# Loading w_in by half chunks, and a reordered start, in a float32 attention and feed-forward kernel

## The chip, the cores and the metric

The kernel runs on one core of one Trainium2 chip. The metric is the device time of one execution in microseconds (us), as the median of several runs. Engines are named as in the profile: PE is the matrix engine (PEld its weight loads), DVE the vector engine, ACT the scalar engine, POOL GpSimd, SP the queue that issues all DMAs here.

## The reference

A cross attention between tokens `x` (8 batches, 8 heads, 512 tokens, head size 64) and 32 state rows per head, in both directions, and then a feed-forward block on all 8 x 544 rows:

```
a  = softmax(scale * x @ state.T);   xread = a @ state        # 512 rows per batch
a2 = softmax(scale * state @ x.T);   sread = a2 @ x           # 32 rows per batch
y  = concat([xread, sread]) -> (4352, 512)
h  = y @ w_in                        # w_in  (512, 2048)
g  = h / (1 + exp(-1.702 h))
out = g @ w_out                      # w_out (2048, 512), out float32
```

`x` and `state` are float32. The weights arrive as 64-bit floating point numbers, so `w_in` is 8 MiB and each weight has to be turned into a float32 number on the chip.

## The kernel before

**What the matrix engine does.** Since `xread = a @ state`, the kernel never forms `xread`. For a batch b and a chunk c of 512 of the 2048 hidden columns it forms `M(b, c)`, the product of the state and of `w_in`'s chunk (`att_M`, L451: eight small matmuls that run beside each other, then two ACT copies out of PSUM, L460). `up_x(b, f)` (L529, `up` L520) multiplies 128 columns of M with the transposed softmax `aT` of the batch; ACT applies the activation (L527, "gelu" below). Four `up_x` use one chunk. Batches 0 and 1 are made this way at the start, chunk by chunk, while the weights still come in; the down projection and the other six batches follow, and the change leaves their order as it is.

**Pieces of weights.** `w_in` is loaded in 16 pieces of 512 KB (`PIECES` L166, `load_weight` L170): in chunk c, piece k is the 128 rows k of 512 columns, 4 KB a row. 16 pieces of `w_out` follow. A piece is turned into float32 by five DVE instructions and two on ACT: `mask` (L207) takes the exponent's bits; the "powers" or clamps (L218 and L219) are two ACT instructions on it; then DVE's `fraction` (L225), L236 (which needs the powers), L239 and L243. `powers_to(n)` brings masks and powers up to piece n, `round_to(n)` does the rest up to piece n and runs powers some pieces ahead. M(b, 0) needs the first four pieces, M(b, 1) the next four, and so on. Below, p0 to p15 are the pieces in order.

**The order.** The schedule is manual: each engine, and SP's queue of DMAs, runs its instructions in the order in which the code emits them (L1124 and below). SP issues p0 and p1, the state and x of batch 0, p2 and p3, the state and x of batch 1, then p4 and on. PE begins with `keep_warm` (L122: matmuls on zeros whose result nobody reads), turns x of batch 0 (`att_xT_arriving`), makes its scores, runs 24 more such matmuls, turns state and x of batch 1 (`att_state`, `att_xT`: 4 transposes of PE and an ACT copy for each of four head pairs), makes batch 1's scores (`att_scores`, L343), then M(0, 0), four `up_x` of batch 0, M(1, 0), four of batch 1, M(0, 1), and so on. The softmax of batch 0 is DVE's `att_x_norm(0)` (L403 to L408), which ends in `aT(0)`. That of batch 1 is `att_blocks(1)` (L351), `att_x_exp(1)` (L394, L395 and an exponential on ACT, L396) and `att_x_norm(1)`. Between exponentials and gelus ACT loads another table of functions (ACT_TABLE_LOAD).

**Buffers.** PSUM tiles come from two pools with two buffers each: "att" (transposes, most M) and "h" (`up_x`, warm matmuls; with `spare=True` M takes "h" and `up_x` takes "att"). A matmul group waits until ACT has read the tile that held its buffer.

Of the kernel before, what the change touches and what calls it, by code (L numbers as in the profile page):

```python
# [10 lines left out]
FP32 = mybir.dt.float32  # L11
I32 = mybir.dt.int32
U32 = mybir.dt.uint32
AF = mybir.ActivationFunctionType
# [6 lines left out]
def kernel(  # L21
# [30 lines left out]
    nc = tc.nc  # L52

    B, H, S, D = x.shape
# [3 lines left out]
    P = 128  # L58
    NPR = P // Ns
    NG = H // NPR  # L60
    NF = DF // P
    SCH = S // P
    ST = S + Ns
    FC = 512
    NFC = DF // FC
# [16 lines left out]
    mpool = ctx.enter_context(tc.tile_pool(name="mpool", bufs=1))  # L82
# [4 lines left out]
    psH = ctx.enter_context(tc.tile_pool(name="psH", bufs=2, space=bass.MemoryType.PSUM))  # L87
# [4 lines left out]
    def att_ps(shape, name):  # L92
        return psA.tile(shape, FP32, tag="att", name=name)
# [16 lines left out]
    low = konst.tile([P, 6, S], FP32, name="low")  # L110
# [11 lines left out]
    def keep_warm(n):  # L122
        ps = psH.tile([P, FC], FP32, tag="h", name="warm")
        for _ in range(n):
            nc.tensor.matmul(ps, zeros[:, :P], zeros, start=True, stop=True)  # L125
# [9 lines left out]
    def load_x(b):  # L135
        if b == 1:
            xn[b] = sums[:, 0].rearrange("p (c h d) -> p c h d", c=SCH, h=H)
        else:
            xn[b] = xpool.tile([P, SCH, H, D], FP32, tag="xn", name=f"xn_{b}")
        for c in range(SCH):  # L140
            nc.sync.dma_start(xn[b][:, c], x_v[b, c])
# [20 lines left out]
    w_in = [konst.tile([P, NPR, FC], FP32, name=f"w_in_{c}") for c in range(NFC)]  # L162
    w_out = konst.tile([P, NF, DM], FP32, name="w_out")
    w_in_words, w_out_words = moe_w_in.bitcast(I32), moe_w_out.bitcast(I32)

    PIECES = [("i", c, k) for c in range(NFC) for k in range(NPR)] + [("o", f) for f in range(NF)]  # L166
    raw, power, begun = {}, {}, {}
    AHEAD = 3

    def load_weight(i):  # L170

        key = PIECES[i]
        nin, room = NFC * NPR, NF // 2
        if i < room or nin - NPR <= i < nin:
            o = 2 * (i % room if i < room else i - (nin - NPR))
            raw[i] = w_out[:, o : o + 2].rearrange("p f n -> p (f n)").bitcast(I32)
        else:
            o = 2 * (i % 4)
            raw[i] = later[:, o : o + 2].rearrange("p f n -> p (f n)").bitcast(I32)
        if key[0] == "i":  # L180
            _, c, k = key
            src = w_in_words[P * k : P * (k + 1), 2 * FC * c : 2 * FC * (c + 1)]
        else:
            src = w_out_words[P * key[1] : P * (key[1] + 1)]
        nc.sync.dma_start(raw[i], src)

# [4 lines left out]
    for i, v in enumerate((8.0 * most, 8.0 * (most - least))):  # L193
        t = konst.tile([P, 1], FP32, name=f"edge_{i}")
        nc.gpsimd.memset(t, v)
        edge.append(t)

    def words(i):
        w = raw[i].rearrange("p (n w) -> p w n", w=2)
        return w[:, 0].bitcast(U32), w[:, 1]  # L200

    def mask(i):

        _, hi = words(i)
        sc = low[:, 2 + i % (AHEAD + 1)].bitcast(I32)
        power[i] = sc
        nc.vector.tensor_scalar(sc, hi, 0x7FF00000, None, ALU.bitwise_and)  # L207

    def round_a(i):
# [3 lines left out]
        sc = power[i]  # L213
        if PIECES[i][0] == "o":
            nc.vector.tensor_scalar(sc, sc, most, least, ALU.min, ALU.max)
# [5 lines left out]
    def fraction(i):  # L221

        key = PIECES[i]
        dst = w_in[key[1]][:, key[2]] if key[0] == "i" else w_out[:, key[1]]
        nc.vector.tensor_scalar(dst.bitcast(I32), words(i)[1], 0xFFFFF, 0x100000, ALU.bitwise_and, ALU.bitwise_or)  # L225
        begun[i] = dst

# [19 lines left out]
    def before(i):  # L247

        nin = NFC * NPR
        return i - (nin - NPR if i < nin else 2 * NPR if i < nin + NPR else NPR)  # L250

    def load_weights(upto):
        while done["load"] < min(upto, len(PIECES)):
            load_weight(done["load"])
            done["load"] += 1

    def powers_to(n):
        while done["a"] < min(n, len(PIECES)):
            load_weights(done["a"] + 1)
            round_a(done["a"])  # L260
            done["a"] += 1

    def round_to(n, ahead=AHEAD):

        nin = NFC * NPR
        while done["b"] < min(n, len(PIECES)):
            i = done["b"]
            powers_to(i + 1)
            round_b(i, min(i + 1 + ahead, max(nin, i + 1)), i + 1 < nin and (i + 1 < n or i >= NPR))
            done["b"] += 1  # L270
            while done["b"] > NPR and done["load"] < len(PIECES) and before(done["load"]) < done["b"]:
                load_weights(done["load"] + 1)
# [12 lines left out]
    A = {b: {} for b in range(B)}  # L285
# [29 lines left out]
    def by_state(b, ps, rhs):  # L315

        for j in range(NPR):
            for g in range(NG):
                rows, st = slice(D * g, D * (g + 1)), slice(Ns * j, Ns * (j + 1))
                nc.tensor.matmul(ps[g][st], A[b]["stT"][rows, st], rhs(rows, j), start=True, stop=True)  # L320
# [19 lines left out]
    def att_scores(b):  # L340
        a = A[b]
        a["s"] = bank_o[:NG] if b == 0 else bank_o[NG:]
        by_state(b, a["s"], lambda rows, j: a["xT"][rows, j])  # L343
# [54 lines left out]
    def att_x_norm(b):  # L398

        a = A[b]  # L400
        t = a["e1"].rearrange("p g i n -> p (g i) n")
        sm = apool.tile([P, NS1], FP32, tag="sm", name=f"sm_{b}")
        nc.vector.reduce_sum(out=sm, in_=t, axis=AX.X)  # L403
        nc.vector.tensor_scalar(sm, sm, eps, None, ALU.add)
        nc.vector.reciprocal(out=sm, in_=sm)
        nc.vector.tensor_tensor(out=t, in0=t, in1=sm.to_broadcast((P, NS1, Ns)), op=ALU.mult)
        a["aT"] = low[:, :NG] if b == 1 else apool.tile([P, NG, S], FP32, tag="aT", name=f"aT_{b}")
        nc.vector.transpose(  # L408
            a["aT"].rearrange("p g t -> p (g t)"), a["e1"].rearrange("p g i n -> p (g i n)")
        )  # L410
# [37 lines left out]

    turns = {"M": 0}

    def att_M(b, c, spare=False):  # L451

        m = mpool.tile([P, NG, FC], FP32, tag=f"M{turns['M'] % NFC if b < 2 else c}", name=f"M_{b}_{c}")
        turns["M"] += 1
        A[b]["M", c] = m
        name = f"M_{b}_{c}_"
        ps = [psH.tile([P, FC], FP32, tag="h", name=name + str(g)) if spare else att_ps([P, FC], name + str(g)) for g in range(NG)]
        by_state(b, ps, lambda rows, j: w_in[c][rows, j])
        for g in range(NG):
            nc.scalar.copy(m[:, g], ps[g])  # L460


    squares = dram.tile([Ns, NG * NB, NPR, Ns], FP32, name="squares")
# [53 lines left out]

    G = {}

    def up(key, f, ntok, lhs, rhs, spare=False):  # L520
        hps = att_ps([P, ntok], f"h_{key}_{f}") if spare else psH.tile([P, ntok], FP32, tag="h", name=f"h_{key}_{f}")
        n = len(lhs)
        for i in range(n):
            nc.tensor.matmul(hps, lhs[i], rhs[i], start=(i == 0), stop=(i == n - 1))  # L524
        if f % 2 == 0:
            G[key, f // 2] = free.pop(0)
        nc.scalar.activation(out=G[key, f // 2][:, f % 2, :ntok], in_=hps, func=AF.Gelu_apprx_sigmoid)  # L527

    def up_x(b, f, spare=False):  # L529
        c, o = divmod(P * f, FC)  # L530
        m = A[b]["M", c]
        up(b, f, S, [m[:, g, o : o + P] for g in range(NG)], [A[b]["aT"][:, g] for g in range(NG)], spare)

    O = {}

# [582 lines left out]
    nper = FC // P  # L1118

    def rounds(n):  # L1120
        round_to(done["b"] + n)
# [2 lines left out]
    load_weights(2)  # L1124
    load_state(0)
    load_x(0)
    load_weights(NPR)
    load_state(1)
    load_x(1)
    load_weights(2 * NPR)  # L1130
    keep_warm(16)
    powers_to(1)
# [5 lines left out]
    powers_to(3)  # L1138
    nc.scalar.activation(out=A[0]["e1"], in_=A[0]["e1"], func=AF.Exp, scale=scale)
    att_scores(0)  # L1140
    powers_to(2)
    round_to(3, 0)
    powers_to(4)
    att_x_norm(0)
    keep_warm(24)
    att_state(1)
    for j in range(NPR):
        keep_warm(2)
        att_xT(1, j)
    att_scores(1)  # L1150
    keep_warm(3)
    powers_to(4)
    round_to(NPR, 1)
    att_M(0, 0)
    powers_to(NPR + 2)


    att_blocks(1)
    att_x_exp(1)
    up_x(0, 0)  # L1160
    up_x(0, 1)
    up_x(0, 2, True)
    up_x(0, 3, True)

    att_M(1, 0, True)
    round_to(NPR + 1)
    att_x_norm(1)

    def turn(b, c, then, n=()):

        for i in range(nper):
            if i == nper - 1 and then:
                att_M(*then)
            up_x(b, nper * c + i)
            if i < len(n):
                rounds(n[i])

    turn(1, 0, None, [1, 1, 1])
    att_M(0, 1)
    turn(0, 1, (1, 1), [1, 1, 1])  # L1180
    round_to(3 * NPR)
    turn(1, 1, (0, 2), [1, 1])
    round_to(4 * NPR)
# [80 lines left out]
    for b in range(1, B):  # L1264
# [25 lines left out]
        k = 3 if b + 1 < B else 0  # L1290
# [40 lines left out]
```

## Time and profile before

| What | Value |
|---|---|
| median of 9 runs (lowest to highest) | 710.52 us (710.4 to 710.63) |
| profiled execution: own time, span | 710.4 us, 708.6 us |
| PE busy | 696.2 us (98%) |
| DVE busy | 602.5 us (85%) |
| ACT busy | 231.2 us (33%) |
| granted PE clock | 0.998 |
| DMA engines busy, 10 to 20, 20 to 30, 30 to 40, 40 to 50 us | 0.99, 1.00, 0.55, 0.22 |
| DVE busy in 10 us, from 20, 30, 40, 50, 60, 70 us | 9.76, 9.86, 10.00, 10.00, 9.72, 5.75 |
| ACT busy in 10 us, from 20, 30, 40, 50 us | 6.92, 8.31, 8.28, 9.20 |

A line of the timeline reads: start in us, length in us, engine, line of the code, operation, tile written <- tiles read, shape, count; in brackets the idle time of the engine before it and what ended it. The chain of waits is the work that ended last, followed back from the end, in order of time: start, length, engine, tile and line; "issue" is time in which nothing visible was waited for. A float32 matmul has two records.

### The profile page before, as it was taken

What the parts mean: (1) busy time and instruction counts of PE and PEld (TensorE: products, weight loads), DVE (VectorE), ACT (ScalarE), POOL (GpSimd) and SP (SyncE); (2) the same over time, 40 slices, a digit from 0 to 9 for tenths busy, and PEclk for the clock granted to TensorE, in tenths of its full rate; (3) what the DMA queues carried; (4) which work ended last, traced back from release to release, by engine and by line L of the source; (5) the groups of instructions that cost most, each with busy time, mean ns of one, the idle gap of its engine ahead of it and who ended that gap; (6) DMA issues with size and microseconds to landing.
All of it is one profiled execution on the core that took longest, in us unless ns stands there. A gap on an engine that the chain in (4) does not pass through costs nothing.

```text
span 708.6 us, 12669 instructions
## 1 busy us (share of the span) xinstructions
PE 696.2 (98%) x4975; PEld 557.3 (79%) x4975; DVE 602.5 (85%) x1246; ACT 231.2 (33%) x456; POOL 0.8 (0%) x8
## 2 busy tenths in 40 slices
PE   8989999999999999999999999999999999999996
PEld 3433444458998799879998899889987998899995
DVE  6999799999978998799978997899789987888650
ACT  5686510114224412423233423341243224300210
POOL 0000000000000000000000000000000000000000
PEclk9999999999999999999999999999999999999999
DMA  9921246328842384409550665147432850041001
GB/s 233 363 78 51 95 146 144 121 78 204 209 123 46 59 196 136 79 1 193 164 108 1 140 190 119 20 79 194 140 54 43 197 150 16 0 118 63 16 1 29
DMA packets 143914, 77.89 MB, mean 110 GB/s; under 512 B 113904, under 2 KB 127728, under 8 KB 143856
## 3 DMA queue, kind: packets, MB, share of 16 engines
q1 hardware_dynamic: 143856, 77.09, 41.9%
q8 instruction: 39, 0.64, 0.4%
q14 instruction: 19, 0.16, 0.1%
HBM read 61.08 MB, written 15.99 MB: 109 GB/s over the span
## 4 chain that ended last, share of the span: by engine, by line
PE 95%; ACT 2%; DMA 2%; SPq 0%; DVE 0%; issue 0%; DVEq 0%; ACTq 0%
PE low L689 21%; PE o L1051 17%; PE o L738 14%; PE o L689 10%; PE o L542 8%; PE h L524 7%; PE upx L1051 6%; PE M L320 4%; PE o L585 2%; PE o L320 1%; PE sr L500 1%; PE warm L125 1%; PE upx_sr L1051 1%; DMA out_dram<-osb_sr 1%; DMA xn<-in_x_dram 1%; ACT low L219 1%
## 5 line engine op out<-in xcount | busy, mean ns | idle before, releaser
L1061 DVE TENSOR_TENSOR g<-o,g 128x512 f32<-128x512 f32 (+1 forms) x140 | 88.0, 650 | 51.1 <-PE o L1051 50.2
L738 PE MATMUL o<-w_out,g 128*128 128x256 f32 x448 | 100.5, 380 | 0.0
L738 PEld LDWEIGHTS o<-w_out,g 128*128 128x128 f32 x448 | 84.2, 190 | 16.9 <-issue 5.5
L1058 ACT ACTIVATE g<-g 128x512 f32<-128x512 f32 (+1 forms) x84 | 49.8, 600 | 100.8 <-DVE g L1061 100.8
L1051 PE MATMUL upx<-aT,M 128*128 128x256 f32 x192 | 49.3, 379 | 0.0
L1051 PE MATMUL o<-ta,M 128*128 128x256 f32 x192 | 49.3, 379 | 0.0
L1051 PE MATMUL o<-ta,ms 128*128 128x256 f32 x192 | 48.3, 379 | 0.0
L689 PE MATMUL low<-low,g 128*128 128x128 f32 x336 | 44.4, 275 | 0.0
L460 ACT COPY M<-M 128x512 f32<-128x512 f32 x64 | 33.2, 596 | 28.2 <-PE M L320 28.2
L689 PEld LDWEIGHTS low<-low,g 128*128 128x128 f32 x336 | 40.9, 192 | 0.0
L1051 PEld LDWEIGHTS o<-ta,ms 128*128 128x128 f32 x192 | 36.5, 190 | 5.0
L1051 PEld LDWEIGHTS o<-ta,M 128*128 128x128 f32 x192 | 36.5, 190 | 5.0
L1051 PEld LDWEIGHTS upx<-aT,M 128*128 128x128 f32 x192 | 36.0, 190 | 4.6
L689 PE MATMUL low<-sums,later 128*128 128x128 f32 x280 | 37.0, 275 | 0.0
L689 PEld LDWEIGHTS low<-sums,later 128*128 128x128 f32 x280 | 34.6, 192 | 0.4
L320 PE MATMUL M<-w_in,stT 64*32 64x512 f32 x512 | 32.7, 594 | 0.2 <-ACT eT L490 0.2
L524 PE MATMUL h<-low,M 128*128 128x512 f32 x64 | 29.7, 600 | 1.4 <-DVE low L408 1.4
L524 PE MATMUL h<-aT,M 128*128 128x512 f32 x64 | 28.7, 599 | 1.4 <-ACT M L460 1.4
L689 PE MATMUL low<-w_out,g 128*128 128x128 f32 x224 | 29.6, 275 | 0.0
L527 ACT ACTIVATE g<-h 128x512 f32<-128x512 f32 x24 | 14.0, 591 | 45.1 <-PE h L524 45.1
L542 PE MATMUL o<-w_out,g 128*128 128x512 f32 x64 | 28.7, 594 | 0.0
L542 PE MATMUL o<-w_out,sums 128*128 128x512 f32 x64 | 28.6, 594 | 0.0
(210 smaller groups left out, 1294.3 us busy)
## 6 DMA issues: line engine op xcount, KB each, us to landing
low<-low SPq DMA_DIRECT2D x78, 256.0 KB, 3.4
later<-in_moe_w_out_dram SPq DMA_DIRECT2D x16, 512.0 KB, 3.3
xn<-in_x_dram SPq DMA_DIRECT2D x28, 256.0 KB, 4.7
low<-low SPq DMA_DIRECT2D x9, 768.0 KB, 4.0
w_out<-in_moe_w_in_dram SPq DMA_DIRECT2D x12, 512.0 KB
xsq<-in_x_dram SPq DMA_DIRECT2D x96, 64.0 KB, 2.4
out_dram<-osb SPq DMA_DIRECT2D x18, 256.0 KB, 2.8
out_dram<-later SPq DMA_DIRECT2D x14, 256.0 KB, 2.2
```

Source lines behind the costliest of these rows:

```text
L125: nc.tensor.matmul(ps, zeros[:, :P], zeros, start=True, stop=True)
L320: nc.tensor.matmul(ps[g][st], A[b]["stT"][rows, st], rhs(rows, j), start=True, stop=True)
L460: nc.scalar.copy(m[:, g], ps[g])
L524: nc.tensor.matmul(hps, lhs[i], rhs[i], start=(i == 0), stop=(i == n - 1))
L527: nc.scalar.activation(out=G[key, f // 2][:, f % 2, :ntok], in_=hps, func=AF.Gelu_apprx_sigmoid)
L542: nc.tensor.matmul(ops, G[key, f // 2][:, f % 2, P * r : P * (r + 1)], w_out[:, f], start=(f == 0), stop=(f == NF - 1))
L585: nc.tensor.matmul(ps[:, r], lhs[f][:, P * r : P * (r + 1)], rhs[:, f], start=(first and r == 0 and f == 0), stop=(f == HF - 1), skip_grou ...
L689: nc.tensor.matmul(ps, lhs[f], rhs[:, f], start=(first and f == 0), stop=(f == QF - 1), skip_group_check=True)
L738: nc.tensor.matmul(ps[:, r], lhs[f][:, P * r : P * (r + 1)], rhs[:, f], start=(r == 0 and f == 0), stop=(f == HF - 1), skip_group_check=True,)
L1051: nc.tensor.matmul(ps[:, k], lhs[i][:, o : o + P], rhs[i], start=(first and k == 0 and i == 0), stop=(i == n - 1), skip_group_check=True,)
L1058: nc.scalar.activation(out=dst, in_=src, func=AF.Gelu_apprx_sigmoid)
L1061: nc.vector.tensor_tensor(out=dst, in0=ps, in1=x, op=ALU.add)
```

## The change

`w_in`'s pieces keep their size but change their shape: a piece is now two row blocks (256 rows) by 256 columns, rows of 2 KB. The first two pieces of a chunk are its left 256 columns, the last two its right ones. `att_M` can be made by halves (`h=0`, `h=1`), and `up_x` can hold its gelu back until `gelus()`. The start is reordered: p3 is loaded behind x of batch 1 instead of ahead of it; the left half of M(0, 0) is made right after batch 0's scores; 12 warm matmuls are run in place of 24 and 3; after batch 1's scores come `up_x(0, 0)` and `up_x(0, 1)` with their gelus held, then batch 1's exponential, then the gelus, the rounding of p3, the right half of M(0, 0) and M(1, 0). Powers of p4 and p5 now follow M(1, 0)'s copies instead of preceding batch 1's exponential, `att_x_norm(1)` precedes the rounding of p4, M(0, 1) is made by halves, and copies of M are emitted ahead of a piece's powers. DVE's and ACT's instructions on a piece, of `w_out` too, see it as two rows of 256 instead of one of 512; their number and their elements stay as they are.

```
-    PIECES = [("i", c, k) for c in range(NFC) for k in range(NPR)] + [("o", f) for f in range(NF)]
+    PIECES = [("i", c, h, k) for c in range(NFC) for h in range(2) for k in range(2)] + [("o", f) for f in range(NF)]
...
-            _, c, k = key
-            src = w_in_words[P * k : P * (k + 1), 2 * FC * c : 2 * FC * (c + 1)]
+            _, c, h, k = key
+            n0 = 2 * FC * c + FC * h
+            src = w_in_words[2 * P * k : 2 * P * (k + 1), n0 : n0 + FC].rearrange("(k p) n -> p k n", k=2)
+            nc.sync.dma_start(raw[i].rearrange("p (k n) -> p k n", k=2), src)
...
-    def att_M(b, c, spare=False):
+    def att_M(b, c, spare=False, h=None):
...
+        n0, n = (0, FC) if h is None else (FC // 2 * h, FC // 2)
...
+        by_state(b, ps, lambda rows, j: w_in[c][rows, j, n0 : n0 + n])
         for g in range(NG):
-            nc.scalar.copy(m[:, g], ps[g])
+            nc.scalar.copy(m[:, g, n0 : n0 + n], ps[g])
...
+    def gelus():
+        for out, hps in held:
+            nc.scalar.activation(out=out, in_=hps, func=AF.Gelu_apprx_sigmoid)
+        held.clear()
...
-    load_weights(NPR)
+    load_weights(NPR - 1)
     load_state(1)
     load_x(1)
+    load_weights(NPR)
     load_weights(2 * NPR)
...
     att_scores(0)
+    att_M(0, 0, h=0)
     powers_to(2)
     round_to(3, 0)
     powers_to(4)
     att_x_norm(0)
-    keep_warm(24)
+    keep_warm(12)
     att_state(1)
...
     att_scores(1)
-    keep_warm(3)
-    powers_to(4)
-    round_to(NPR, 1)
-    att_M(0, 0)
-    powers_to(NPR + 2)
+    up_x(0, 0, hold=True)
+    up_x(0, 1, hold=True)
     att_blocks(1)
     att_x_exp(1)
-    up_x(0, 0)
-    up_x(0, 1)
+    gelus()
+    round_to(NPR, 0)
+    att_M(0, 0, h=1)
+    att_M(1, 0, True)
+    powers_to(NPR + 2)
     up_x(0, 2, True)
     up_x(0, 3, True)
-    att_M(1, 0, True)
+    att_x_norm(1)
     round_to(NPR + 1)
-    att_x_norm(1)
 
     def turn(b, c, then, n=()):
         for i in range(nper):
-            if i == nper - 1 and then:
+            up_x(b, nper * c + i)
+            if i == nper - 2 and then:
                 att_M(*then)
-            up_x(b, nper * c + i)
             if i < len(n):
                 rounds(n[i])
 
-    turn(1, 0, None, [1, 1, 1])
-    att_M(0, 1)
-    turn(0, 1, (1, 1), [1, 1, 1])
+    turn(1, 0, (0, 1, False, 0), [1, 1, 1])
+    up_x(0, nper)
+    att_M(0, 1, h=1)
+    rounds(1)
+    up_x(0, nper + 1)
+    rounds(1)
+    up_x(0, nper + 2)
+    att_M(1, 1)
+    rounds(1)
+    up_x(0, nper + 3)
     round_to(3 * NPR)
```

More of the change, by code (lines that the diff above doesn't have):

```diff
@@ L180, in load_weight @@
         if key[0] == "i":
-            _, c, k = key
-            src = w_in_words[P * k : P * (k + 1), 2 * FC * c : 2 * FC * (c + 1)]
-        else:
-            src = w_out_words[P * key[1] : P * (key[1] + 1)]
-        nc.sync.dma_start(raw[i], src)
+            _, c, h, k = key
+            n0 = 2 * FC * c + FC * h
+            src = w_in_words[2 * P * k : 2 * P * (k + 1), n0 : n0 + FC].rearrange("(k p) n -> p k n", k=2)
+            nc.sync.dma_start(raw[i].rearrange("p (k n) -> p k n", k=2), src)
+        else:
+            nc.sync.dma_start(raw[i], w_out_words[P * key[1] : P * (key[1] + 1)])
     least, most = float((1023 - 127) << 20), float((1023 + 128) << 20)
@@ L196, with halved @@
         edge.append(t)
+    def halved(t):
+        return t.rearrange("p (k n) -> p k n", k=2)
     def words(i):
-        w = raw[i].rearrange("p (n w) -> p w n", w=2)
+        w = raw[i].rearrange("p (k n w) -> p w k n", k=2, w=2)
         return w[:, 0].bitcast(U32), w[:, 1]
@@ L204, in mask @@
         _, hi = words(i)
-        sc = low[:, 2 + i % (AHEAD + 1)].bitcast(I32)
+        sc = halved(low[:, 2 + i % (AHEAD + 1)]).bitcast(I32)
         power[i] = sc
@@ L223, in fraction @@
         key = PIECES[i]
-        dst = w_in[key[1]][:, key[2]] if key[0] == "i" else w_out[:, key[1]]
+        if key[0] == "i":
+            _, c, h, k = key
+            dst = w_in[c][:, 2 * k : 2 * k + 2, FC // 2 * h : FC // 2 * (h + 1)]
+        else:
+            dst = halved(w_out[:, key[1]])
         nc.vector.tensor_scalar(dst.bitcast(I32), words(i)[1], 0xFFFFF, 0x100000, ALU.bitwise_and, ALU.bitwise_or)
@@ L449 @@
     turns = {"M": 0}
-    def att_M(b, c, spare=False):
[L453 to L458, printed above, removed]
+    def att_M(b, c, spare=False, h=None):
+        if not h:
+            A[b]["M", c] = mpool.tile([P, NG, FC], FP32, tag=f"M{turns['M'] % NFC if b < 2 else c}", name=f"M_{b}_{c}")
+            turns["M"] += 1
+        m = A[b]["M", c]
+        n0, n = (0, FC) if h is None else (FC // 2 * h, FC // 2)
+        name = f"M_{b}_{c}_{h}_"
+        ps = [psH.tile([P, n], FP32, tag="h", name=name + str(g)) if spare else att_ps([P, n], name + str(g)) for g in range(NG)]
+        by_state(b, ps, lambda rows, j: w_in[c][rows, j, n0 : n0 + n])
         for g in range(NG):
-            nc.scalar.copy(m[:, g], ps[g])
+            nc.scalar.copy(m[:, g, n0 : n0 + n], ps[g])
     squares = dram.tile([Ns, NG * NB, NPR, Ns], FP32, name="squares")
@@ L518, with up @@
     G = {}
-    def up(key, f, ntok, lhs, rhs, spare=False):
+    held = []
+    def gelus():
+        for out, hps in held:
+            nc.scalar.activation(out=out, in_=hps, func=AF.Gelu_apprx_sigmoid)
+        held.clear()
+    def up(key, f, ntok, lhs, rhs, spare=False, hold=False):
         hps = att_ps([P, ntok], f"h_{key}_{f}") if spare else psH.tile([P, ntok], FP32, tag="h", name=f"h_{key}_{f}")
@@ L526, in up, with up_x @@
             G[key, f // 2] = free.pop(0)
-        nc.scalar.activation(out=G[key, f // 2][:, f % 2, :ntok], in_=hps, func=AF.Gelu_apprx_sigmoid)
-    def up_x(b, f, spare=False):
+        held.append((G[key, f // 2][:, f % 2, :ntok], hps))
+        if not hold:
+            gelus()
+    def up_x(b, f, spare=False, hold=False):
         c, o = divmod(P * f, FC)
         m = A[b]["M", c]
-        up(b, f, S, [m[:, g, o : o + P] for g in range(NG)], [A[b]["aT"][:, g] for g in range(NG)], spare)
+        up(b, f, S, [m[:, g, o : o + P] for g in range(NG)], [A[b]["aT"][:, g] for g in range(NG)], spare, hold)
     O = {}
@@ L1150 @@
     att_scores(1)
-    keep_warm(3)
-    powers_to(4)
-    round_to(NPR, 1)
-    att_M(0, 0)
-    powers_to(NPR + 2)
+    up_x(0, 0, hold=True)
+    up_x(0, 1, hold=True)
     att_blocks(1)
     att_x_exp(1)
-    up_x(0, 0)
-    up_x(0, 1)
+    gelus()
+    round_to(NPR, 0)
+    att_M(0, 0, h=1)
+    att_M(1, 0, True)
+    powers_to(NPR + 2)
     up_x(0, 2, True)
     up_x(0, 3, True)
-    att_M(1, 0, True)
+    att_x_norm(1)
     round_to(NPR + 1)
-    att_x_norm(1)
     def turn(b, c, then, n=()):
         for i in range(nper):
-            if i == nper - 1 and then:
+            up_x(b, nper * c + i)
+            if i == nper - 2 and then:
                 att_M(*then)
-            up_x(b, nper * c + i)
             if i < len(n):
                 rounds(n[i])
-    turn(1, 0, None, [1, 1, 1])
-    att_M(0, 1)
-    turn(0, 1, (1, 1), [1, 1, 1])
+    turn(1, 0, (0, 1, False, 0), [1, 1, 1])
[8 more added lines that the diff above has]
+    up_x(0, nper + 3)
     round_to(3 * NPR)
```

## The prediction

> **What bounds the kernel now.** I read the page first: PE is busy 98% of the span and carries the chain that ended last.
>
> ```profile
> PE 696.2 (98%) x4975; PEld 557.3 (79%) x4975; DVE 602.5 (85%) x1246; ACT 231.2 (33%) x456; POOL 0.8 (0%) x8
> PE 95%; ACT 2%; DMA 2%; SPq 0%; DVE 0%; issue 0%; DVEq 0%; ACTq 0%
> ```
>
> So the time is PE's remaining work plus the moment from which PE no longer waits. That moment lies in the start, hence next the chain of waits in order of time, to 50 us (start, length, engine, tile, line):
>
> ```profile
> 13.21 1.52 PE o L320 x32
> 14.74 5.29 PE warm L125 x24
> ...
> 25.33 0.75 PE warm L125 x3
> 26.09 1.16 PE M L320 x16
> ...
> 27.86 7.13 PE h L524 x16
> 34.99 1.13 PE M L320 x16
> 36.12 1.05 ACT M L460 x2
> ...
> 45.48 0.48 ACT g L527
> 45.96 0.48 ACT M L460
> 46.45 0.04 issue
> 46.49 5.42 PE h L524 x12
> ```
>
> Between 14.74 and 26 us PE mostly runs warm matmuls. From M(0, 0) at 26.02 it works with three holes: 0.75 us ahead of 27.86 (copies of M), 1.44 us ahead of 37.45 (`aT(1)`), 0.68 us ahead of 46.49 (copies of M(0, 1), at the end of an ACT queue without a gap from 36.1 on). From 46.49 PE is full. The hoped-for gain is an earlier 46.49; the marks I compare are there and at M(0, 2), on PE at 60.05, after which both kernels do the same work. Last the timeline, for who releases whom:
>
> ```profile
> 10.60 5.67 SPq L141 DMA_DIRECT2D sums<-in_x_dram  x4
> ...
> 18.56 0.42 DVE L207 TENSOR_SCALAR low<-w_out 128x512 int32<-128x512 int32 x1
> 18.90 1.21 DVE L403 TENSOR_REDUCE sm<-e 128x32 f32<-128x1024 f32 x1
> 19.01 0.72 ACT L218 ACTIVATE low<-low,edge 128x512 f32<-128x512 int32 x1 [1.50 <-DVE low L207]
> ...
> 19.77 0.72 ACT L219 ACTIVATE low<-low,edge 128x512 int32<-128x512 f32 x1
> ...
> 20.40 0.24 ACT L291 COPY stT<-stT 128x128 f32<-128x128 f32 x1
> ```
>
> The reader is to see a row of dominoes: the mask of p3 (18.56) stands on DVE ahead of batch 0's softmax, p3's powers stand on ACT ahead of the copies of batch 1's state and x. It does not wait today, since p3 landed at 15.10 us by the trace's completion records.
>
> **The load that moves.** The same records give p2 13.55, x of batch 1 16.37, 17.80, 18.82 and 19.50, p4 23.34. The engines move bytes in issue order (DMA share 0.99 from 10 to 20 us), so x gains what p3 took, 13.55 to 15.10: 1.55 us. Packets of w_in halve to 2 KB; the trace has 84 ns for one of 2 KB (median, other tensors) and 159 for 4 KB, so a piece takes 16 x 84 instead of 8 x 159 ns on each engine, 0.07 us more; bounds 0 and, by the 166 ns of the slowest tenth, 1.4 us; I take 0.07, the median. Three pieces ahead: x lands at 19.50 - 1.55 + 0.2 = 18.15. p3 is then the first piece behind x. Two rows show how long such a piece takes after x's last landing: p2 after x of batch 0 (11.51 to 13.55), 2.04 us, and p4 after x of batch 1, 3.84. With 0.07 p3 lands at 20.3 to 22.1; the same bytes before it can't be through before 19.5 + 0.3 = 19.8. I take the middle, 21.2, 2.6 us after DVE wants it. Call this landing L. Queued behind the waiting mask: on DVE all of batch 0's softmax, on ACT behind p3's powers every copy of batch 1, and PE behind those copies for want of PSUM.
>
> **The walk from L** (durations from the rows above and their neighbours). On DVE mask to end of `aT(0)` took 18.56 to 23.25: `aT(0)` at L + 4.7. On ACT the mask's start to the copy of the state took 1.84: L + 1.9. PE has run its 12 warm matmuls (0.22 us each, to 18) and batch 1's first transposes and now waits. From there the four copies of x go at the pace of 0.87 us of today (two warm matmuls, four transposes), the first without its wait: last copy ends at L + 5.1; the last scores took 1.1 us after it: L + 6.2 (today 25.33). Now PE runs `up_x(0, 0)` and `(0, 1)`, 1.72 us each (0.43 a record): L + 6.2 to L + 9.6. On DVE, L351 to L395 take 3.82 (26.07 to 29.89): the exponential starts on ACT at L + 10.1 (today 29.93), takes 1.06, the table 1.28, two gelus 1.1: L + 13.6. Meanwhile DVE rounds p3 in 2.35 (as p2, 16.29 to 18.64): L + 12.4; the right half of M(0, 0) follows on PE (0.67, as the 256-column scores at 10.79) and has ended when ACT is free; its copies take 0.6 (0.59 at 512 columns, 0.25 at 128: 0.36 each, overlapping by 0.1). PE idles from L + 9.6 to L + 12.6. M(1, 0) needs the two PSUM buffers that the held gelus free: L + 13.6 to L + 14.7, copies 1.07: L + 15.8. Then ACT has no gap: a piece's powers take 1.40 and a gelu 0.48 (37.06 to 40.31). Powers of p4 and p5, two gelus, powers of p6 and p7: the gelu of `up_x(1, 0)` at L + 22.3, although PE began that `up_x` at L + 18.0 (`aT(1)` L + 17.3). `up_x(1, 2)` waits for its buffer from L + 21.5 to L + 22.9. Powers of p8, gelu, powers of p9, gelu: copies of the left half of M(0, 1) at L + 26.5, and `up_x(0, 4)` starts at L + 26.9. From here PE is full: the right half of M(0, 1) (0.45), M(1, 1) (0.95), seven `up_x` (12.04): M(0, 2) at L + 40.4.
>
> **The sum.** L + 40.4 against 60.05: the change costs L - 19.65 us, +1.55 at L = 21.2. In other terms: the exponential starts 1.4 us later, the ACT queue behind it up to `up_x(0, 4)` is 16.8 instead of 16.56 us, and half of M(0, 1) is still to be made. The three old holes do go; what is late instead is ACT, which now does the powers of p4 and p5 (2.8 us; before, they lay beside idle ACT at 24.53 and 28.18) between the exponential and the gelus.
>
> What costs nothing, and why: p4 and later pieces land some 0.3 us later (four and more times 0.07), p4 at 23.6, which DVE asks for at L + 12.4. Pieces p4 to p15 get done about 4.3 us later on DVE (p4 at L + 20.5 instead of 33.04, then 2.33 to 2.45 each), but M(0, 2)'s are done 3 us and M(0, 3)'s 2 us before PE wants them. Further on DVE has one hole, 3.87 us ahead of L378 at 73.89; it shrinks to about 1, and whatever is later than that on DVE adds to the time. Elements per instruction stay, so two rows of 256 for one of 512 are priced at 0 (bounds 0 and one more 0.1 us gap per instruction on DVE, which the same hole covers up to 1 us). If a half of M should wait for pieces of the other half (it reads the same tile), the left half of M(0, 1) waits for p6, L + 25.4, not p5: up to 0.8 us. I take 0; the trace of before shows no such case.
>
> On the profiled execution (710.4 us, span 708.6 and 1.8 around it) this gives 711.95; the median is 0.12 above that execution: 712.1.
>
> [...] In the trace the first ten warm matmuls start 0.43 us apart and the next ones 0.22, the granted clock being 1.00 all along, and no hole over 1.5 us follows. [...] By the trace alone it stays 712.1.
>
> **The rivals.** (1) PE comes back at half pace. It idles from about 19.4 (the warm matmuls emitted ahead of the wait) to L + 2.2 = 23.4, 4 us, and from L + 9.6, 3 us. For it: the half pace at the start, 4.2 us long, so a price of up to 2.1 us of PE work. After the first hole the second one hides it; after the second, PE's wait of 1.4 us for a buffer hides part: 0.7 to 2.1 us more, 712.8 to 714.2. Against it: no row of before shows PE slowing down again. (2) Rows of 2 KB, 16 KB apart and in two blocks, come slowly from memory. At the slowest tenth's 166 ns the four pieces up to p3 take 1.4 us more each, and p0 and p1 lie ahead of x of batch 0, on which the start waits (8.25): at least 2.8 us, 714.9 and up. Against it: the medians. (3) Not slower: p3 is no gate. If it lands by 18.56, as late as DVE could ask, the same walk gives 18.56 - 19.65 = -1.1 us, 709.4; the rival decides against me below L = 19.65. The most that closing all three old holes could bring is 2.9 us, 707.6. For it: p4's late landing is that of a few lagging engines, and the order of transfers is judged from completions. Against it: 1 MB of x in 256-byte rows now stands ahead of p3, and it alone lands between 16.37 and 19.50 today.
>
> **How the numbers follow.** The forecast has a chance of 0.57, with a range of its own from 710.7 (L = 19.8) to 713.8 (L = 22.1 and the 0.8 us); rival 1 0.17, rival 2 0.08, rival 3 0.18. For 8 in 10 I leave out rival 2, the top of rival 1 and the gains beyond 709.3: 709.3 to 714.2. What a measurement here can tell is 0.2%, 1.4 us: the upper half of the forecast and rivals 1 and 2 are slower, 0.52; the lower half and half of rival 3 are the same, 0.40; faster 0.08.
>
> **What would show it.** Right: DVE's L207 ahead of L403 idle for 2 to 3 us on a DMA; ACT's L218 and batch 1's copies that much later; the exponential (L396) at about 31.3; `up_x(0, 4)` at 48.1; M(0, 2) at 61.6. Wrong: L207 without a wait, the exponential before 29.8, M(0, 2) before 60. Rival 1 shows in the starts of `up_x(0, 0)` 0.86 us apart; rival 2 in 2 KB packets over 100 ns and a first x transpose after 9 us.

## The result, and the profile after

The changed kernel takes 713.15 us (median of 9 runs, 711.76 to 715.06) against 710.52: a ratio of 1.004, 95% interval 1.0031 to 1.0048, so 2.6 us slower. The profiled execution took 713.15 us, its span is 711.4 and its granted clock 0.996.

First the page of the kernel after, busy time and shares of the chain:

```profile
PE 696.3 (98%) x4992; PEld 557.1 (78%) x4992; DVE 602.6 (85%) x1246; ACT 231.1 (32%) x460; POOL 0.8 (0%) x8
...
PE 93%; ACT 2%; SPq 2%; DMA 2%; DVE 1%; issue 0%; DVEq 0%; ACTq 0%
```

PE is busy as long as before (696.2). Its share of the chain has fallen from 95% to 93%, and SP's queue and DVE have come in: the start waits longer. Where it waits is in the chain of waits of the kernel after (start, length, engine, tile, line):

```profile
14.60 5.62 DMA w_out<-in_moe_w_in_dram
20.22 0.02 issue
20.24 0.44 DVE low L212
20.70 0.73 ACT low L223
21.46 0.72 ACT low L224
22.18 0.16 ACT stT L300
22.34 0.04 issue
22.39 0.66 PE xT L308 x4
...
25.86 1.96 PE o L329 x16
27.82 1.31 DVE e L360 x2
...
31.66 1.06 ACT e L405
...
44.38 1.98 PE h L542 x4
...
62.90 1.02 PE M_None L329 x16
```

The lines of the code are new: the mask is L212 (before L207), the powers L223 and L224, the exponential L405, `up` L542. The reader is to see the row of dominoes: p3's transfer is now on the chain to 20.22, then its mask, its powers, the copy of batch 1's state, and only then PE. M(0, 2) is the last line, and in the chain of the kernel before it is

```profile
60.11 1.02 PE M L320 x16
```

So it starts 2.79 us later; the rest of the execution, 710.4 - 60.11 = 650.29 before and 713.15 - 62.90 = 650.25 after, is the same, and the whole difference lies ahead of M(0, 2). (The timeline puts M(0, 2) 0.07 us earlier than the chain, at 60.05 and 62.83; below, numbers of one view are compared with each other.)

The timeline of the kernel after shows who waited, the second of the three lines on PE:

```profile
20.24 0.43 DVE L212 TENSOR_SCALAR low<-w_out 128x512 int32<-128x512 int32 x1 [1.67 <-DMA w_out<-in_moe_w_in_dram]
22.39 0.66 PE L308 MATMUL xT<-ident,sums 128*128 128x128 f32 x4 [2.65 <-ACT stT L300]
23.95 1.06 PE L125 MATMUL warm<-sums 128*128 128x512 bf16 x2
```

The mask waits 1.67 us for the load, PE 2.65 us for ACT. The third line is a second loss: two warm matmuls there take 1.06 us; two such took 0.59 at 22.88. The table by windows of 2 us (us, PE, PEld, DVE and ACT busy, POOL, granted clock, DMA share, GB/s) says why:

```profile
20.00:22.00 2.00, 0.00 (x0) 0.00 (x0) 1.72 (x3) 1.26 (x2) 0.00 (x0) 1.00 0.87 285
22.00:24.00 2.00, 1.61 (x11) 1.35 (x12) 1.90 (x4) 1.41 (x4) 0.00 (x0) 0.88 1.00 314
24.00:26.00 2.00, 2.00 (x13) 1.19 (x17) 0.94 (x1) 0.69 (x2) 0.00 (x0) 0.50 1.04 396
26.00:28.00 2.00, 2.00 (x17) 0.48 (x6) 0.20 (x1) 0.48 (x1) 0.00 (x0) 0.76 1.04 400
28.00:30.00 2.00, 2.00 (x6) 0.82 (x5) 1.97 (x3) 0.00 (x0) 0.00 (x0) 1.00 1.06 392
```

The granted clock is 0.88, 0.50 and 0.76 in three windows: 0.24 + 1.00 + 0.48 = 1.72 us of full-speed PE time is missing. The trace's own clock records give the stretch exactly: half pace from 23.53 us for 3.41 us, which is 1.71 us of PE work. It begins after PE has resumed (22.39). This **clock fall** is not in every execution. By mean granted clock the executions fall into three groups: 0.998 took 711.76 to 712.85 us, 0.996 took 713.09 to 713.37, 0.994 took 714.47 to 715.06. One fall is 1.71 of 711 us, 0.0024 of the mean clock, and both traces also end at half pace (3.3 us of it before, 1.8 us here), so that an execution without a fall reads 0.998 to 1.0: the groups are what no fall, one and two would give. The profiled execution has one, and it is the median.

### The profile page after: what moved, and what is told of

Same layout as the page of the kernel before. It is cut to its first block, busy times and chain, and to the rows that moved or that the text cites. A ratio compares the mean times of both kernels' runs of the same rounds, so it can differ in the third digit from the quotient of the medians.

```text
span 711.4 us, 12713 instructions
## 1 busy us (share of the span) xinstructions
PE 696.3 (98%) x4992; PEld 557.1 (78%) x4992; DVE 602.6 (85%) x1246; ACT 231.1 (32%) x460; POOL 0.8 (0%) x8
## 4 chain that ended last, share of the span: by engine, by line
PE 93%; ACT 2%; SPq 2%; DMA 2%; DVE 1%; issue 0%; DVEq 0%; ACTq 0%
PE low L709 21%; PE o L1071 17%; PE o L758 14%; PE o L709 10%; PE o L562 8%; PE h L542 7%; PE upx L1071 6%; PE M_None L329 4%; PE o L605 2%; SPq L141 1%; PE sr L511 1%; PE o L329 1%; PE upx_sr L1071 1%; DMA out_dram<-osb_sr 1%; DMA w_out<-in_moe_w_in_dram 1%; ACT low L224 1%
## 5 line engine op out<-in xcount | busy, mean ns | idle before, releaser
L471 ACT COPY M<-M_None 128x512 f32<-128x512 f32 x60 | 31.1, 597 | 27.1 <-PE M_None L329 27.1
L542 PE MATMUL h<-low,M 128*128 128x512 f32 x64 | 30.1, 600 | 1.1 <-ACT g L535 1.1
L329 PE MATMUL M_None<-w_in,stT 64*32 64x512 f32 x480 | 30.7, 594 | 0.3 <-ACT eT L501 0.2
L542 PE MATMUL h<-aT,M 128*128 128x512 f32 x64 | 29.1, 600 | 0.0
```

The source lines that it names most:

```text
L471: nc.scalar.copy(m[:, g, n0 : n0 + n], ps[g])
```

## The experiments

Theory: the reordered load makes p3 late, p3's mask and powers stand ahead of batch 1's start on DVE and ACT, and the wait that this opens on PE sometimes costs a clock fall besides. Rivals: the new shape of the pieces; more powers between exponential and gelus on ACT; the reorder itself. Each kernel was timed beside the kernel before (710.53, 710.5 and 710.57 us in the three groups of runs).

**The load order alone** (the kernel before with p3 behind x of batch 1, pieces unchanged):

```
-    load_weights(NPR)
+    load_weights(NPR - 1)
     load_state(1)
     load_x(1)
+    load_weights(NPR)
```

> The kernel before with the new order of loads alone (p3 behind batch 1's x). Theory: mask of p3 waits until about 20.2 us and all behind it shifts by 1.7 us; PE has its 24 warm matmuls until 20, so its clock holds: 711.9 to 712.4 us. Rival (a late p3 is taken up by the slack behind it): 710.5 as before.

Measured: 712.24 us, ratio 1.0025 [1.0016, 1.0035]. The timeline of that kernel (with the old line numbers):

```profile
20.27 0.43 DVE L207 TENSOR_SCALAR low<-w_out 128x512 int32<-128x512 int32 x1 [1.47 <-DMA w_out<-in_moe_w_in_dram]
22.41 0.66 PE L299 MATMUL xT<-ident,sums 128*128 128x128 f32 x4 [0.83 <-ACT stT L291]
39.20 7.11 PE L524 MATMUL h<-low,M 128*128 128x512 f32 x16 [1.73 <-DVE low L408]
```

The mask waits for p3 just as in the change, and one moved load costs 1.7 us. PE waits only 0.83 us ahead of the transposes (24 warm matmuls fill the rest); every execution has a mean clock of 0.999 or 1.0.

**The shape alone** (the kernel before with pieces of two row blocks by 256 columns, in the old order of loads):

```
-            src = w_in_words[P * k : P * (k + 1), 2 * FC * c : 2 * FC * (c + 1)]
+            n0 = 2 * FC * c + FC * h
+            src = w_in_words[2 * P * k : 2 * P * (k + 1), n0 : n0 + FC].rearrange("(k p) n -> p k n", k=2)
...
```

> The kernel before with the new shape of pieces alone (two row blocks by 256 columns, rows of 2 KB; M still waits for all four pieces of a chunk). Theory: a piece takes about as long as before (in the changed kernel the first two landed at 4.5 and 6.0 us, before at 4.7 and 6.1), and two rows of 256 cost DVE and ACT nothing: 710.3 to 710.9 us. Rival (rows of 2 KB or the split rows are part of the loss): over 711.3.

Measured: 710.3 us, ratio 0.9997 [0.9988, 1.0006]. The shape, rows of 2 KB and instructions on two rows of 256, costs nothing that can be told.

**The mask later** (the change with p3's mask and powers moved behind batch 1's scores, so that nothing of batch 1's start stands behind them):

```
     round_to(3, 0)
-    powers_to(4)
     att_x_norm(0)
...
     att_scores(1)
+    powers_to(4)
     up_x(0, 0, hold=True)
```

> The changed kernel with one move: mask and powers of the fourth piece (p3) stand behind batch 1's scores instead of ahead of batch 0's softmax. Theory (p3's late landing holds DVE and ACT, PE goes cold in the wait): no wait of DVE ahead of batch 0's softmax, copies of batch 1 from 18.3 instead of 22.1 us, PE idle under 1.5 us and its granted clock 1.00 from 20 to 30 us, batch 1's exponential at about 28.0 instead of 31.66, so 3.6 us off: 709.2 to 709.9 us, with runs within 0.5 us of each other. Rival (what costs is ACT's order, the powers of p4 and p5 between the exponential and the gelus): the exponential comes earlier, but the time stays above 711.5.

Measured: 709.84 us, ratio 0.9988 [0.9979, 0.9997], 3.3 us less than the change. The timeline of that kernel:

```profile
18.96 0.33 PE L308 MATMUL xT<-ident,sums 128*128 128x128 f32 x1 [0.19 <-DMA sums<-in_x_dram]
22.73 0.38 DVE L212 TENSOR_SCALAR low<-w_out 128x512 int32<-128x512 int32 x1
27.51 1.06 ACT L405 ACTIVATE e<-e 128x1024 f32<-128x1024 f32 x1 [2.89 <-DVE e L404]
29.80 0.64 PE L329 MATMUL M<-w_in,stT 64*32 64x256 f32 x8 [1.98 <-DVE w_in L252]
```

The mask at 22.73 waits for nothing; the exponential starts at 27.51 instead of 31.66, M(0, 2) at 58.75. p3 is loaded as late as in the change, so it is not the late load by itself that costs, but what stands behind its mask in order. The time is as expected, the spread is not: 708.7 to 710.34 us where 0.5 us was expected. A PE hole of 1.98 us remains ahead of the right half of M(0, 0), and seven of the eleven executions have a mean clock of 0.996 or 0.997, that of one fall.

**Warm matmuls while p3 is awaited** (the change with the hole of 2.65 us filled; PE's work is the same otherwise):

```
-        keep_warm(2)
+        keep_warm(15 if j == 1 else 2)
```

> The changed kernel with 13 more warm matmuls in PE's wait for the copies of batch 1 (15 instead of 2 ahead of the second head pair). Theory (the wait slows PE's clock, which costs 1.2 us and makes the runs differ): granted clock 1.00 from 20 to 30 us, batch 1's scores end at 26.6 instead of 27.8 us, 711.7 to 712.2 us, runs within 0.6 us of each other where they were 3.3 us apart. Rival (the spread and the slow stretch come from the transfers, p3 landing at varying times): the spread stays over 2 us and the median at 713.

Measured: 712.31 us (712.05 to 712.98), ratio 1.0027 [1.0016, 1.0037]. Its timeline on DVE, ACT and PE:

```profile
20.43 0.43 DVE L212 TENSOR_SCALAR low<-w_out 128x512 int32<-128x512 int32 x1 [1.79 <-DMA w_out<-in_moe_w_in_dram]
30.58 1.06 ACT L405 ACTIVATE e<-e 128x1024 f32<-128x1024 f32 x1 [4.99 <-DVE e L404]
24.89 1.80 PE L329 MATMUL o<-xT,stT 64*32 64x512 f32 x16
32.86 0.64 PE L329 MATMUL M<-w_in,stT 64*32 64x256 f32 x8 [1.98 <-DVE w_in L252]
47.63 1.88 PE L542 MATMUL h<-aT,M 128*128 128x512 f32 x4
61.75 0.66 PE L329 MATMUL M_None<-w_in,stT 64*32 64x512 f32 x8
```

p3's mask starts at 20.43 there, 0.2 us later than in the change, and yet the scores start at 24.89 instead of 25.79 and M(0, 2) at 61.75 instead of 62.83. The clock is 1.00 from 20 to 30 us, where it was 0.83. From the copy of the state (22.27 here, 22.09 in the change) to the end of the scores it is 4.42 us against 5.68: of the fall's 1.71 us, 1.26 reached the path. On the medians, falls make 0.84 us of the loss. The spread is 0.9 instead of 3.3 us, where 0.6 was expected; the two slowest of the eight executions have a mean clock of 0.996 and 0.997.

**p3 ahead again** (the change with only the load order undone):

```
-    load_weights(NPR - 1)
+    load_weights(NPR)
     load_state(1)
     load_x(1)
-    load_weights(NPR)
```

> The changed kernel with the old order of loads (p3 ahead of batch 1's state and x), all else as changed. Theory: mask of p3 without a wait at 18.5 us, its powers from 19.0, copies of batch 1 from 20.4, the exponential at about 29.3, 710.2 to 711.0 us. Rival (the order of loads is harmless): 713 as the changed kernel.

Measured: 711.03 us (710.03 to 711.56), ratio 1.0006 [0.9997, 1.0015]. The timeline of the second hole on PE:

```profile
30.85 0.86 PE L329 MATMUL M<-w_in,stT 64*32 64x256 f32 x8 [1.98 <-DVE w_in L252]
```

and the windows around it:

```profile
30.00:32.00 2.00, 1.15 (x9) 0.33 (x10) 1.97 (x5) 1.99 (x4) 0.00 (x0) 0.78 1.05 386
32.00:34.00 2.00, 2.00 (x17) 0.27 (x15) 1.90 (x4) 0.56 (x3) 0.00 (x0) 0.50 1.04 384
34.00:36.00 2.00, 2.00 (x8) 1.02 (x5) 1.97 (x3) 1.86 (x4) 0.00 (x0) 0.86 0.96 353
```

The mask does not wait for a DMA (18.42), and 2.1 us of the loss are gone. The exponential starts at 28.57, still 1.06 us behind the kernel with the mask later: that edit saves the wait for p3 and, besides, the time that mask and powers themselves take ahead of batch 1's start. What the reorder gains with p3 in place, a fall takes back: this time after the hole of 1.98 us, and again 0.44 + 1.00 + 0.28 = 1.72 us. The two executions at a mean clock of 0.998 took 710.03 us, the others, at 0.996 to 0.997, 710.96 to 711.56.

**Powers early** (the change with mask and powers of p4 and p5 back ahead of batch 1's softmax, to take 2.8 us out of ACT's queue between exponential and gelus):

```
+    powers_to(NPR + 2)
     att_blocks(1)
...
     att_M(1, 0, True)
-    powers_to(NPR + 2)
```

> The changed kernel with masks and powers of p4 and p5 ahead of batch 1's exponential again, where DVE idles 2.9 and ACT 5.2 us. Theory (these powers delay the gelus that free PE's buffers): PE's wait of 1.1 to 1.9 us ahead of the third up_x of batch 1 goes, and about 1 us of the time: 711.8 to 712.4. Rival (ACT's order costs nothing, only the landing of p3 and the clock do): 713 as the changed kernel.

Measured: 714.4 us (five executions, 712.66 to 714.99), ratio 1.0053 [1.004, 1.0065]: this expectation failed. The timeline on PE:

```profile
37.30 4.98 PE L542 MATMUL h<-aT,M 128*128 128x512 f32 x8
46.18 1.98 PE L542 MATMUL h<-low,M 128*128 128x512 f32 x4 [0.47 <-ACT g L535]
```

The hole ahead of `up_x(1, 2)` did shrink, from 1.07 to 0.47 us. But the profiled execution has two falls (granted clock 0.83 in both 20 to 30 and 30 to 40 us), and eight records of `up_x` took 4.98 instead of 3.70 us. So this run could not tell the order of ACT's queue from the clock; the two kernels with fills below do.

**Mask later and powers early together** (both edits):

> The mask and powers of p3 behind batch 1's scores (as in e1) and those of p4 and p5 ahead of batch 1's exponential (as in e6). Theory: e1's 709.8 less PE's wait for the third up_x's buffer (1.2 us), but DVE now waits for p5, which lands at about 23.8, ahead of batch 1's blocks, 0.5 to 0.8 us more: 708.9 to 709.6 us. Rival (in e1 DVE sets the pace, and masks ahead of the blocks lose what ACT gains): 709.8 or more.

Measured: 709.8 us (708.27 to 711.0), ratio 0.9989 [0.998, 0.9997], the same as the mask later alone, and the rival's number. The timeline on DVE and PE:

```profile
24.17 0.43 DVE L212 TENSOR_SCALAR low<-w_out 128x512 int32<-128x512 int32 x1 [0.52 <-DMA w_out<-in_moe_w_in_dram]
33.54 4.70 PE L542 MATMUL h<-aT,M 128*128 128x512 f32 x8
```

Asked this early, p5 has not landed, and its mask delays the softmax behind it (exponential at 28.36 instead of 27.51); and after the second hole, 2.70 us here, came a fall (granted clock 0.83 from 30 to 40 us). The three executions at 0.998 and more took 708.27 to 708.71, less than the four such with the mask later (708.7 to 710.34); the eight with a fall took 709.37 to 711.0, against 709.55 to 710.13. So this run does not decide between theory and rival.

**Mask later, the second hole warmed**:

```
+    ps = att_ps([P, FC], "warm")
+    for _ in range(10):
+        nc.tensor.matmul(ps, zeros[:, :P], zeros, start=True, stop=True)
     att_M(0, 0, h=1)
```

> e1 with 10 warm matmuls in PE's second hole, ahead of the right half of M(0, 0) (in a PSUM buffer of the other pool). Theory (the runs of e1 from 708.7 to 710.3 differ by PE's clock after the holes): all runs near e1's fastest, 708.6 to 709.1, within 0.5 us of each other. Rival (e1's spread comes from the transfers): median 709.8 and a spread over 1 us.

Measured: 709.01 us (708.58 to 709.55), ratio 0.9978 [0.9969, 0.9987]. One row of its table by windows:

```profile
20.00:30.00 10.00, 10.00 (x60) 4.37 (x61) 9.33 (x14) 5.71 (x8) 0.00 (x0) 1.00 1.05 392
```

PE has no hole left there, the mean clock is 0.999 or 1.0 in every execution, and the spread is 1.0 instead of 1.6 us (0.5 was expected). The median falls by 0.8 us although M(0, 2) starts at 58.71, as in the profile with the mask later (58.75): that profile happened to have no fall.

**Both holes of the change filled**, with the powers behind M(1, 0) as in the change, and with them early (both fills as in the diffs above):

> The changed kernel with both of PE's holes filled by warm matmuls (15 ahead of state and x of batch 1, 10 ahead of the right half of M(0, 0)), mask of p3 left where the change put it. Clock theory: the granted clock is 1.00 in every 10 us from 20 to 60 and the runs agree within 0.6 us; M(0, 2) as with the first hole filled alone, 61.8; 712.0 to 712.3. If the second hole costs time by itself: under 711.8.

> As the kernel with two fills, and mask and powers of p4 and p5 ahead of batch 1's softmax: the order that cost time with the holes open (714.4), now with the clock held. Theory A, ACT's queue behind the exponential is a term and the earlier loss was the clock's: clock 1.00, M(0, 2) 0.9 to 1.1 us earlier than with two fills alone, 711.0 to 711.3. Theory B, early powers cost time whatever the clock: 712.3 or more.

Measured: 712.13 us (711.54 to 712.9), ratio 1.0021 [1.0012, 1.003], and 711.39 us (711.0 to 712.66), ratio 1.0013 [1.0004, 1.0022]; the clock is 1.00 in every 10 us from 20 to 60 in both. PE ahead of `up_x(1, 2)`, first with the powers behind:

```profile
42.98 1.98 PE L542 MATMUL h<-low,M 128*128 128x512 f32 x4 [1.07 <-ACT g L535]
61.43 1.09 PE L329 MATMUL M_None<-w_in,stT 64*32 64x512 f32 x16
```

then with the powers early:

```profile
42.85 1.98 PE L542 MATMUL h<-low,M 128*128 128x512 f32 x4 [0.47 <-ACT g L535]
61.29 1.09 PE L329 MATMUL M_None<-w_in,stT 64*32 64x512 f32 x16
```

With the clock held, ACT's order is worth 0.74 us on the medians; the trace shows 0.60 of it as the hole that shrinks. M(0, 2) itself is only 0.14 earlier, because p3's mask starts 0.47 later in the second profile (20.57 instead of 20.10). The spreads are 1.4 and 1.7 us although every execution has a mean clock of 0.998 or more: by that they are not the clock's, and how far landings of p3 make them was not measured. The expected 0.6 us of spread and 711.0 to 711.3 were too hopeful. Filling the second hole of the change brought 0.2 us on the median, within the intervals: in the change's own profile it had no fall.

**The best version: mask later, second hole warmed, powers of p4 alone early** (p5 not asked before it has landed):

```
+    powers_to(NPR + 1)
     att_blocks(1)
```

> The mask-later kernel with its second hole warmed, and mask and powers of p4 alone ahead of batch 1's softmax instead of behind M(1, 0)'s copies (those of p5 stay behind). Theory A, ACT's queue between the exponential and the gelus is what leaves PE its last hole, 1.07 us ahead of up_x(0, 4): one piece's powers less in that queue (1.40 us), the hole closes, M(0, 2) at 57.7 in place of 58.71, 708.0 us in place of 709.0. Theory B, mask and powers taken early delay the exponential, because p4 lands only at 22 to 23 us: M(0, 2) at 58.7 or later, 709.0 to 709.6.

Measured: 708.49 us (707.86 to 709.4), ratio 0.9973 [0.9963, 0.9982]. On PE:

```profile
38.98 1.98 PE L542 MATMUL h<-low,M 128*128 128x512 f32 x4 [0.47 <-ACT g L535]
57.43 1.09 PE L329 MATMUL M_None<-w_in,stT 64*32 64x512 f32 x16
```

The hole is 0.47 us where it was 1.07, as with two pieces early, and did not close as theory A had it: four powers (of p6 and p7) still lie between the two gelus ahead of it. M(0, 2) is 1.21 us earlier than in the profile of the version before (58.64 in its timeline), but only 0.60 of that is the hole: the other 0.61 is there at the exponential already (26.86 against 27.47). In the version before, the chain of waits runs through the landing of x of batch 1 at 18.87; in this execution it does not. It beats both kernels, by 2.1 and 4.7 us; the version before it is 0.5 us slower on the median, but the intervals overlap, so the times do not show what the last step gains.

## Why the prediction came out as it did

**The sign and the mechanism were right.** p3 is the gate: the load order alone (+1.7 us) and the mask later (-3.3) show it from both sides. "DVE's L207 ahead of L403 idle for 2 to 3 us on a DMA" was 1.67, less than said; the exponential "at about 31.3" was 31.66; `up_x(0, 4)` "48.1" was 48.71; "M(0, 2) at 61.6" was 62.83. The number 712.1 lies among the executions without a fall (711.76 to 712.85), and on that of the two fills, 712.13. That it comes so near is luck: behind it, sizes are off that cancel.

- **L, taken as 21.2, was 20.22.** x of batch 1 came at 18.9 instead of 18.15, and p3 1.3 us behind it, where the two rows that I took it from gave 2.04 and 3.84. By the instructions that waited for the two, it came 1.49 us behind with the first hole filled (20.43 and 18.94) and 1.35 with powers early (20.57 and 19.22). Why the two rows were longer no run shows. Effect on the sum: -1.0 us.
- **The walk from L to the exponential, 10.1 us, was right with the clock held:** mask at 20.43, exponential at 30.58 in the kernel with the first hole filled, 10.15.
- **ACT's queue from the exponential to `up_x(0, 4)`, 16.8 us,** was 17.05 there (47.63 - 30.58): +0.25. ACT did become what is late next, as foreseen, and early powers win 0.7 us.
- **From `up_x(0, 4)` to M(0, 2), 13.5 us, was 14.12** (61.75 - 47.63): +0.6. In the chain of after, half of M(0, 1) kept PE 0.59 us, not 0.45, and M(1, 1) 1.02, not 0.95; that leaves 12.51 for the seven `up_x`, 1.79 each, not the 1.72 that I made from the spacing of their records. The chain of before had the right row, 7.13 us for four.
- **The clock: rival 1 (0.17) happened, in part and elsewhere.** Its hole was 2.65 us, not 4. I wrote that after the first hole "the second one hides it". That is the step that failed: the slow stretch, from 23.53 to 26.94, lay in the transposes and the scores, and the scores release DVE's softmax and with it the exponential, so the hole behind them moved along and hid nothing; 1.26 us reached M(0, 2). `up_x(0, 0)`, where I would have looked for it, ran at full pace. (The 1.00 that I read over the slow first warm matmuls of the kernel before was no measurement: its clock records begin only at 5.57 us.)
- **Terms at nothing:** shape and instructions on two rows are confirmed (710.3). That left half of M(0, 1) waited for no piece of the other half: it starts at 46.37 right behind `up_x(1, 2)`. DVE's hole of 3.87 us shrank to 2.01, not to 1, and still covered its delay.
- **Rival 2** (2 KB rows come slowly) is refuted by the shape alone. **Rival 3** (p3 no gate, 709.4) names the right alternative: with the mask later, which makes p3 no gate, 709.84.

In sum, against the forecast's M(0, 2): -1.0 (L) + 0.3 (ACT) + 0.6 (PE) + 1.3 (clock) = +1.2, measured 62.83 - 61.6 = +1.2. Against the kernel before: the load order makes 1.7 us (as it did alone), the clock 0.8, the shape nothing. The reorder's own gain is there, 0.5 us with p3 ahead in the executions without a fall and 1.5 us with the mask later and the hole warmed, but the change spends it by leaving p3's mask ahead of batch 1's start.

How short a hole on PE is safe, the runs do not show. The holes here were 2.65 us (the change) and 1.98 us (p3 ahead), and falls followed them; in the 3.41 us ahead of the change's fall PE was busy for 1.15. That fall begins 17.07 us after the trace's clock records do (6.46), five times its own length. Why the same hole brings a fall in some executions and not in others no run here isolates.

## What to carry to other kernels

When a load moves back, look not at when its data are needed for the result but at which instruction asks for it first, and at everything that is queued behind that instruction on an in-order engine; here, moving p3's mask and its powers back saved 3.3 us, where the moved load alone cost 1.7. Price a hole on the matrix engine by what stands behind the slow stretch too: if other engines wait for that stretch, a later hole does not hide it. And a hole of 2 us that cannot be closed can be worth filling with idle matmuls, for the spread as much as for the median: it gained 0.8 us with the mask later, and nothing that can be told (0.2 us) in the change with its first hole filled.

## What was not expected of the hardware

- The five clock falls in the profiles (one each in the change, with p3 ahead, and with mask later and powers early; two with powers early) cost the same: 1.71 us of PE work by the clock records of the change (3.41 us at half pace), 1.70 to 1.72 by the granted clock of the windows in the others. Each began after PE had resumed, not in the hole: at 23.53 in the change (PE back at 22.39) and, worked out from windows of 2 us, at 31.12 with p3 ahead (30.85) and at 22.84 and 36.48 with powers early (22.71 and 34.68). With mask later and powers early, the half of M(0, 0) right behind the hole, at 30.65, still took 0.64 us, as in the profile of the mask later, which has no fall.
- A hole of 1.98 us was followed by a fall in some profiles (p3 ahead again) and not in others (the mask later, and the second hole of the change, 1.99). The busy time of PE in the 3.41 us ahead gives no plain bound: 0.68 to 1.70 us ahead of these four starts, but 1.60 us in a stretch of the change (30.36 to 33.77) that no fall followed. Mean clocks of 0.998, 0.996 and 0.994 then sort the executions of the change into groups, about 1.0 and 1.4 us apart.
- Halving the rows of a load from 4 KB to 2 KB changed nothing that can be told: 710.3 against 710.5 us.
